# A table for the PSUM banks, the early stage 1 in parts of one pair, 24 single dummy matmuls, and a new order

## The chip, the core and the metric

The kernel runs on one core of a Trainium2 chip. The metric is the time of one execution in microseconds (us), measured on the device; the median over runs counts. The core has five engines that run side by side, each through its own list of instructions in order: PE (TensorE: matmuls, with PEld, the load of the stationary operand, beside it), DVE (VectorE), ACT (ScalarE), POOL (GpSimd) and SP (SyncE, which issues nearly all DMAs here). They wait for each other through semaphores. Matmul results go to PSUM, which has eight banks of 128 x 512 floats; DVE and ACT read them from there.

## The reference

Two layers of attention follow each other, over 8 batches with 576 positions.

```python
scores = scale * np.matmul(q, k.transpose(0, 1, 3, 2))        # 8 heads of 64
mask = (rel >= 0) & (rel < window)                            # window = 64
attn = exp(scores - max); attn /= attn.sum(-1) + 1e-9
x = (attn @ v) laid out as (8, 576, 512)
logits = x @ w_gate                                           # 4 experts, 2 are chosen
for e in range(4):                                            # causal attention of each expert
    a = softmax(scale * (x @ wq[e]) @ (x @ wk[e]).T, causal)
    out += (gate weight of e, or 0) * (a @ (x @ wv[e]) @ wo[e])
```

## The kernel before

**Stage 1** is the windowed attention. Two heads make a pair, so there are 32 pairs, four to a batch. A block of 64 queries sees only its own 64 keys and the 64 before, and eight such blocks of a pair, or of neighbouring pairs, make a unit u; there are 36 units. For a unit, `s1_qk` makes the scores on PE (the tiles s1_u_0 and s1_u_1 in the orders below, two banks), ACT and DVE bring them to SBUF (DVE by `copy_predicated`), DVE takes the row maximum, POOL subtracts it, ACT takes the exponential, DVE the sum and its reciprocal, and POOL multiplies (the tile sm1_u all along, st1_u for maximum, sum and reciprocal). `s1_t` transposes the result on PE (t1_u) and masks it (pt1_u): for the first nine units two of the four masked parts are DVE's and two POOL's, later all four POOL's. `s1_av` multiplies by v on PE (o1_u), and ACT and DVE split the result into a high part xh and a low part xl, so that later products can be made as three fast matmuls. The first 16 blocks come from the first four blocks of each of the four pairs of batch 0, so that the layer behind can begin early.

**Stage 2** is the attention of the experts, two experts at a time (pr = 0, 1). From xh and xl of a batch, PE makes v and the gate's logits (v2ps_b_j), keys and queries (kps_b_pr_half, qps_b_pr_half; 12 matmuls each), then scores (s2_b_pr_k, two banks each), then, after a softmax on DVE, ACT and POOL and a transposition by DVE and DMAs, the product with v (o2_b_pr_part), and last the product with wo (ops_b_j), which ACT or DVE copies out and SP stores. The weights come as 512 KB each and are split by ACT and DVE into parts such as wkhi and wklo before their first use.

**What sets the order.** The functions are first called in an order by planned due times, and each call only records its instructions (`Plan.add`, line 185). A run of matmuls recorded inside one `with nc.block(...)` is one entry; any other instruction is an entry of its own. `Plan.issue` (line 199) then gives the entries out in the order of a table of numbers, `LIST` (lines 29 to 166). All instructions thus have line 203 in the profile. Each engine executes its share of that one order.

**PSUM.** All banks are one pool of eight buffers with one tag. A tile takes the next buffer in turn, in the order in which the functions were called (not the order of `LIST`), and its first matmul waits until the readers of the tile that had the buffer before are done.

**Dummy matmuls.** `warm` (line 540) multiplies the 128 x 128 identity by itself, two matmuls to a call, and there are six calls. The results are not used. They need only `ident`, which POOL makes first.

The change touches `s1_qk` (354), `s1_t` (392), `s1_av` (429), `warm` (540), `s2_v` (546), `proj` (603), `s2_mm` (643), `s2_tp` (714), `s2_av_mm` (778), `s2_o` (808), the pool (225) and the tables.

Of the kernel before, what the change touches and what calls it, by code (L numbers as in the profile page):

```python
# [165 lines left out]
)  # L166
TAIL = 2
WARM = 6
BPOS = 0.05
SJOIN = 1  # L170
PARTS = ((0, 5), (5, 9))
# [797 lines left out]
```

## Time and profile before

| what | value |
|---|---|
| time, median of 3 runs | 412.91 us |
| the runs | 412.62, 412.91, 413.35 us |
| the profiled execution's own time | 413.24 us |
| its span, first to last instruction | 411.5 us |
| PE busy | 398.9 us (97%), 5308 records |
| PEld busy | 358.9 us (87%) |
| DVE busy | 310.7 us (75%) |
| POOL busy | 276.7 us (67%) |
| ACT busy | 260.5 us (63%) |
| moved by DMA | 72.69 MB, 177 GB/s on average |

How to read it: a float32 matmul leaves two records on PE, one of the split parts leaves one. A busy PE is one with a matmul in its pipeline, so short waits between matmuls can hide in it. The time around the span, 413.24 less 411.5 or 1.7 us, is start and end of the execution.

### The profile page before, as it was taken

The page shows a single profiled execution, that of the slowest core. Times are in us where ns is not written, and L with a number is a line of the kernel's source. Part 1 is how long each engine was busy: PE and PEld are TensorE (multiplying, and loading weights), DVE is VectorE, ACT ScalarE, POOL GpSimd, SP SyncE. Part 2 cuts the span into 40 slices and gives each one's busy share as a digit, 9 for nine tenths or more (in the row PEclk, how much of TensorE's full clock was granted, in tenths as well). Part 3 has the DMA queues.
Part 4 walks back from the last instruction along what each step waited for, and adds up shares of the span by engine and source line. Part 5 has one row for each costly group of instructions (what it writes and reads, how often), then busy time and mean ns, then how long its engine had stood idle before and what let it go on. Part 6 is the DMA issues. An engine that isn't in the chain of part 4 may idle for free.

```text
span 411.5 us, 14007 instructions
## 1 busy us (share of the span) xinstructions
PE 398.9 (97%) x5308; PEld 358.9 (87%) x5308; DVE 310.7 (75%) x996; ACT 260.5 (63%) x865; POOL 276.7 (67%) x471
## 2 busy tenths in 40 slices
PE   7689999999999999999999999999999999999996
PEld 7479889999988989898989898988988999898875
DVE  3799998889695878879786876969887768445742
ACT  2666657685748485674858567486856676447852
POOL 3868887977797876887786966877768671504420
PEclk9899999999999999999999999999999999999999
DMA  7987346376867475368776669487657613453113
GB/s 240 349 310 268 111 144 231 78 208 181 239 223 203 135 182 217 106 172 267 193 248 143 205 147 308 130 211 197 176 130 222 151 60 80 131 134 103 53 53 127
DMA packets 33363, 72.69 MB, mean 177 GB/s; under 512 B 6160, under 2 KB 10256, under 8 KB 33296
## 3 DMA queue, kind: packets, MB, share of 16 engines
q1 hardware_dynamic: 32640, 71.14, 58.2%
q8 instruction: 42, 0.69, 0.7%
q10 hardware_dynamic: 656, 0.66, 0.5%
q14 instruction: 25, 0.20, 0.2%
HBM read 39.85 MB, written 9.44 MB: 120 GB/s over the span
## 4 chain that ended last, share of the span: by engine, by line
PE 87%; DVE 8%; POOL 2%; ACT 1%; issue 1%; ACTq 0%; POOLq 0%
PE o L203 18%; PE s L203 17%; PE ops L203 12%; PE v2ps L203 12%; PE kps L203 12%; PE qps L203 11%; PE t L203 4%; DVE pt L203 2%; DVE st L203 2%; DVE sm L203 1%; POOL sm L203 1%; PE warm L203 1%; DVE xl L203 1%; ACT sm L203 0%; DVE wklo L203 0%
## 5 line engine op out<-in xcount | busy, mean ns | idle before, releaser
L203 POOL TENSOR_SCALAR p<-p,r,g 128x448 f32<-128x448 f32 (+4 forms) x135 | 84.0, 636 | 29.5 <-DVE r L203 23.8
L203 POOL TENSOR_TENSOR sm<-sm,st 128x512 f32<-128x512 f32 x72 | 76.9, 1070 | 30.1 <-DVE st L203 20.0
L203 POOL TENSOR_SCALAR_AFFINE_SELECT pt<-ft 64x512 f32<-64x512 f32 x126 | 84.2, 668 | 17.5 <-ACT ft L203 8.4
L203 ACT ACTIVATE p<-p,r 128x192 f32<-128x192 f32 (+3 forms) x135 | 78.7, 588 | 16.9 <-DVE r L203 16.7
L203 PE MATMUL o<-pt,v 128*64 128x64 f32 (+2 forms) x1776 | 80.8, 249 | 1.8 <-DVE pt L203 1.2
L203 PEld LDWEIGHTS o<-pt,v 128*64 128x64 f32 x1776 | 68.2, 138 | 15.0 <-issue 3.2
L203 DVE STREAM_TRANSPOSE st<-p 128x128 f32<-128x128 f32 (+5 forms) x126 | 59.9, 515 | 5.7 <-POOL p L203 5.5
L203 DVE CUSTOM_DVE_ANT_0 p<-s,causal 128x320 f32<-128x320 f32 (+2 forms) x120 | 54.3, 483 | 7.8 <-PE s L203 7.3
L203 DVE TENSOR_REDUCE st<-sm 128x8 f32<-128x512 f32 x72 | 48.4, 679 | 7.0 <-ACT sm L203 6.1
L203 PE MATMUL s<-kt,qt 64*128 64x320 f32 (+3 forms) x480 | 43.3, 318 | 0.0
L203 DVE COPY_PREDICATED sm<-own,s 128x256 f32<-128x256 uint8 x72 | 29.3, 442 | 12.9 <-ACT sm L203 7.7
L203 PE MATMUL kps<-xh,wklo 128*128 128x256 f32 (+1 forms) x128 | 37.7, 295 | 1.2 <-DVE wklo L203 1.2
L203 PE MATMUL kps<-xh,wkhi 128*128 128x256 f32 (+1 forms) x128 | 38.7, 302 | 0.0
L203 PE MATMUL qps<-xh,wqhi 128*128 128x320 f32 (+1 forms) x128 | 38.4, 300 | 0.0
L203 PE MATMUL v2ps<-wvhi,xh 128*128 128x260 f32 x128 | 37.7, 294 | 0.2 <-DVE xl L203 0.2
L203 PE MATMUL s<-k,q 64*64 64x128 f32 (+1 forms) x1116 | 37.8, 275 | 0.1
L203 PE MATMUL qps<-xl,wqhi 128*128 128x320 f32 (+1 forms) x128 | 37.6, 294 | 0.0
L203 PE MATMUL kps<-xl,wkhi 128*128 128x256 f32 (+1 forms) x128 | 37.6, 294 | 0.0
L203 PE MATMUL qps<-xh,wqlo 128*128 128x320 f32 (+1 forms) x128 | 37.6, 294 | 0.0
L203 PEld LDWEIGHTS s<-kt,qt 64*128 64x128 f32 x480 | 35.0, 186 | 2.8 <-issue 0.7
L203 PE MATMUL v2ps<-wvhi,xl 128*128 128x260 f32 x128 | 36.2, 283 | 0.0
L203 PE MATMUL v2ps<-wvlo,xh 128*128 128x260 f32 x128 | 36.2, 283 | 0.0
(124 smaller groups left out, 921.6 us busy)
## 6 DMA issues: line engine op xcount, KB each, us to landing
v<-in_vW_dram SPq DMA_DIRECT2D x28, 576.0 KB, 5.2
pt<-st SPq DMA_DIRECT2D x112, 116.0 KB, 2.3
pt<-st SPq DMA_DIRECT2D x112, 80.0 KB, 2.1
out_dram<-out SPq DMA_DIRECT2D x32, 256.0 KB, 2.5
k<-in_kT_dram SPq DMA_DIRECT2D x28, 288.0 KB, 5.0
q<-in_qT_dram SPq DMA_DIRECT2D x28, 288.0 KB, 5.2
v<-in_vW_dram SPq DMA_DIRECT2D x3, 320.0 KB, 5.9
out_dram<-out SPq DMA_DIRECT2D x7, 128.0 KB, 2.5
```

Of the source, the lines that this page charges most:

```text
L203: call(*args, **kw)
```

## The change

1. The pool has one buffer to a tag and a tag to a bank, and a new table `BANKS` gives the bank's number for each tile, in the order of the calls. `ops` of the last block takes a whole bank and uses half.
2. For the first four units `s1_qk` and `s1_av` record one entry for each pair instead of one for all eight blocks, so that `LIST` can put the parts apart.
3. There are 24 calls of `warm` with one matmul each, instead of six with two.
4. `LIST` is another order of the entries.

```diff
 LIST = (
-    1, 3, 2, 0, 7, 5, 6, 4, 16, 20, 18, 14, 15, 17, 9, 21, 19, 69, 29, 279, 46, 67, 48, 34, 35, 41, 44, 39, 42, 45,
...
+    1441, 1329, 1439, 1391, 1330, 1443, 1251, 1250, 1417, 1393, 1394, 1241, 1309, 1414, 1331, 1310, 1312, 1332, 1311,
...
+BANKS = (
+    "3421040515401232652071113426734076556201052722743234376660505236110176517730416571043232647642412716"
...
-WARM = 6
+WARM = 24
...
-    psum = ctx.enter_context(tc.tile_pool(name="psum", bufs=2, space=PSUM))
+    psum = ctx.enter_context(tc.tile_pool(name="psum", bufs=1, space=PSUM))
+    numbers = iter(BANKS)
+
+    def bank(shape, name):
+        return psum.tile(shape, F32, tag="s" + next(numbers, "0"), name=name)
...
+    def parts(u):
+        t = list(tiles(u))
+        return [[x for x in t if x[2] == p] for p in sorted({x[2] for x in t})] if u < 4 else [t]
+
     def s1_qk(u):
 
-        banks = [psum.tile([128, 4, 128], F32, tag="s", bufs=8, name=f"s1_{u}_{x}") for x in range(2)]
-        with nc.block("s"):
-            for x, j, p, b in tiles(u):
...
+        banks = [bank([128, 4, 128], f"s1_{u}_{x}") for x in range(2)]
+        for group in parts(u):
+            with nc.block("s"):
+                for x, j, p, b in group:
...
     def warm(k):
-        ps = psum.tile([128, 512], F32, tag="s", bufs=8, name=f"warm_{k}")
+        ps = bank([128, 512], f"warm_{k}")
         with nc.block("z"):
-            for i in range(2):
-                nc.tensor.matmul(ps[:, 0:128], lhsT=ident, rhs=ident, start=True, stop=True)
+            nc.tensor.matmul(ps[:, 0:128], lhsT=ident, rhs=ident, start=True, stop=True)
```

In `s1_av` the same loop over `parts(u)` stands around the matmuls. Every other `psum.tile(...)` becomes `bank(...)`. No other instruction is added or taken away.

**The order at the start, on PE.** The first rows of PE before, from the first dummies to the second unit that is multiplied by v:

```order
L203 MATMUL warm_3_103<-ident_85 128x128 x2
L203 MATMUL s1_0_0_106<-k0_74,q0_73 64x64 x2
...
L203 MATMUL warm_4_104<-ident_85 128x128 x2
L203 MATMUL s1_2_0_123<-k0_74,q0_73 64x128 x2
...
L203 MATMUL warm_1_101<-ident_85 128x128 x2
L203 MATMUL t1_0_112<-ident_85,sm1_0_108 128x128 x4
...
L203 MATMUL t1_1_122<-ident_85,sm1_1_115 128x128 x4
L203 MATMUL o1_0_117<-pt1_0_110,v0_79 64x64 x8
L203 MATMUL o1_0_117<-pt1_0_110,v1_80 64x64 x8
L203 MATMUL o1_1_129<-pt1_1_120,v2_81 64x64 x8
L203 MATMUL o1_1_129<-pt1_1_120,st2_69 64x64 x8
L203 MATMUL s1_4_0_146<-st2_69 64x128 x2
```

The same stretch of PE in the changed kernel (k and q are the loaded keys and queries of a pair, v its values, st2 the buffer that holds the fourth pair):

```order
L213 MATMUL warm_18_118<-ident_85 128x128
L213 MATMUL s1_0_0_124<-k0_74,q0_73 64x64 x2
...
L213 MATMUL warm_14_114<-ident_85 128x128
L213 MATMUL s1_3_0_151<-k1_76,q1_75 64x128 x2
L213 MATMUL s1_3_1_152<-k1_76,q1_75 64x128 x2
L213 MATMUL s1_2_1_142<-k1_76,q1_75 64x128 x2
...
L213 MATMUL t1_0_130<-ident_85,sm1_0_126 128x128 x4
...
L213 MATMUL o1_0_135<-pt1_0_128,v1_80 64x64 x8
L213 MATMUL s1_4_0_164<-st2_69 64x128 x2
...
L213 MATMUL t1_2_150<-ident_85,sm1_2_143 128x128 x4
L213 MATMUL o1_1_147<-pt1_1_138,st2_69 64x64 x8
```

Eleven single dummies stand ahead of the first scores where there were eight matmuls, one stands behind unit 0, one inside unit 1, eight behind it and one ahead of t1_0; units 4 and 5, and the transposition of unit 2, have moved ahead of o1_1. Unit 6 and t1_3, not shown, have moved ahead of the first keys (kps).

**The order where DVE last gives PE something to wait for, on PE.** The last matmuls of the first experts' scores and what follows, before (one row of each block; the rest of a block repeats it with other operands):

```order
L203 MATMUL s2_0_0_3_1_250<-kt_0_0_217,qt0_88 128x256
L203 MATMUL v2ps_0_4_268<-wvhi_170,xt0_0_163 128x260
...
L203 MATMUL kps_0_1_1_272<-xh0_118,wkhi_183 128x320
...
L203 MATMUL qps_0_1_1_273<-xh0_118,wqhi_193 128x320
...
L203 MATMUL v2ps_1_1_304<-wvhi_170,xh1_165 128x260
```

And in the changed kernel:

```order
L213 MATMUL kps_0_1_1_290<-xh0_136,wkhi_201 128x320
...
L213 MATMUL s2_0_0_2_0_265<-kt_0_0_235,qt0_88 128x320
...
L213 MATMUL t1_10_0_280<-ident_85,sm1_10_251 128x64
...
L213 MATMUL s2_0_0_3_1_268<-kt_0_0_235,qt0_88 128x256
L213 MATMUL warm_10_110<-ident_85 128x128
L213 MATMUL v2ps_0_4_286<-wvhi_188,xt0_0_181 128x260
...
L213 MATMUL qps_0_1_1_291<-xh0_136,wqhi_211 128x320
...
L213 MATMUL v2ps_1_1_322<-wvhi_188,xh1_183 128x260
```

The second half of the keys (kps_0_1_1), the transposition of unit 10 and one dummy now stand ahead of v2ps_0_4; before, the keys stood right behind it and t1_10 five blocks further on.

**The same place on DVE.** Before, the DVE instructions around the last one that PE has to wait for ahead of v2ps_0_4, which is the copy of unit 11's second bank:

```order
L203 TENSOR_TENSOR gt_0_0_221<-logits0_86,gs_0_0_222 128x16
L203 TENSOR_TENSOR g4_0_0_220<-logits0_86 128x64
L203 COPY_PREDICATED sm1_11_239<-own_82,s1_11_1_238 128x256
L203 ISA p2_1_68,m2_0_0_252<-s2_0_0_2_1_248,causal_98 128x320
L203 ISA m2_0_0_252 128x1
```

In the changed kernel, where the one that v2ps_0_4 waits for is the reading of the scores s2_0_0_2 (the last two rows):

```order
L213 COPY_PREDICATED sm1_11_257<-own_82,s1_11_0_255 128x256
L213 RECIPROCAL st1_10_252<-st1_10_252 128x8
L213 COPY_PREDICATED sm1_11_257<-own_82,s1_11_1_256 128x256
...
L213 COPY_PREDICATED sm1_12_294<-own_82,s1_12_0_292 128x256
...
L213 COPY_PREDICATED sm1_12_294<-own_82,s1_12_1_293 128x256
L213 TENSOR_REDUCE gt_0_0_239<-g4_0_0_238 128x16
L213 ISA p2_1_68,m2_0_0_270<-s2_0_0_2_1_266,causal_98 128x320
L213 ISA m2_0_0_270 128x1
```

Five instructions more stand ahead on DVE: one more copy of unit 11, the two of unit 12, a small reduction of the gate and a reading of scores with its accumulator. The rest of what DVE has done by then is the same in both kernels.

## Rows read from the trace of the kernel before

**Rows 1.** The page's first line.

```profile
span 411.5 us, 14007 instructions
```

**Rows 2.** Windows: stretch and length; busy us of PE, PEld, DVE, ACT, POOL; clock, DMA.

```profile
0.00:10.00 10.00, 7.80 (x103) 7.26 (x105) 3.15 (x12) 2.62 (x7) 3.27 (x20) 1.00 0.79 238
10.00:20.00 10.00, 6.29 (x96) 4.81 (x89) 7.93 (x16) 6.03 (x14) 8.53 (x13) 0.83 0.99 345
20.00:30.00 10.00, 8.19 (x137) 7.53 (x138) 9.88 (x18) 6.60 (x19) 6.50 (x9) 1.00 0.90 342
...
50.00:60.00 10.00, 9.47 (x183) 8.40 (x176) 9.79 (x23) 5.94 (x16) 8.61 (x13) 1.00 0.48 152
```

**Rows 3.** Windows: the stretch from 60 us to 407 us.

```profile
60.00:407.00 347.00, 346.83 (x4460) 312.73 (x4460) 259.88 (x888) 225.28 (x770) 232.62 (x396) 1.00 0.57 164
```

**Rows 4.** Waits of PE, whole span: us in total, times, longest.

```profile
PE t L203 <- POOL sm L203: 3.1, 4, 2.5
PE warm L203 <- POOL ident L203: 2.2, 1, 2.2
PE o L203 <- DVE pt L203: 1.2, 1, 1.2
PE kps L203 <- DVE wklo L203: 1.2, 1, 1.2
...
PE v2ps L203 <- DVE xl L203: 0.2, 1, 0.2
```

**Rows 5.** The chain that ended last, 15 to 60 us: start, length, what.

```profile
24.28 1.55 DVE wklo L203
...
58.25 0.57 DVE xl L203
58.86 1.23 PE v2ps L203 x8
```

**Rows 6.** Waits of DVE between 16 us and 62 us.

```profile
DVE sm L203 <- ACT sm L203: 0.8, 1, 0.8
```

**Rows 7.** Timeline of the first 13 us: start, length, instruction [idle before].

```profile
0.79 0.15 POOL L203 MEMSET sm<- 128x64 f32 x1 [0.29 <-POOLq L955]
...
1.85 0.29 POOL L203 TENSOR_SCALAR_AFFINE_SELECT ident<-ident 128x128 f32<-128x128 f32 x1
...
2.20 3.78 PE L203 MATMUL warm<-ident 128*128 128x128 f32 x16 [2.20 <-POOL ident L203]
...
7.92 0.88 DVE L203 COPY_PREDICATED sm<-own,s 128x256 f32<-128x256 uint8 x2 [2.91 <-PE s L203]
...
9.40 1.26 PE L203 MATMUL s<-k,q 64*64 64x128 f32 x32
...
9.54 0.77 DVE L203 COPY_PREDICATED sm<-own,s 128x256 f32<-128x256 uint8 x2
...
10.60 0.71 PE L203 MATMUL warm<-ident 128*128 128x128 f32 x4
...
12.80 0.64 ACT L203 ACTIVATE sm<-s 128x256 f32<-128x256 f32 x2
```

**Rows 8.** Windows: 14.6 to 18.1 us, with the granted clock third from the end.

```profile
14.60:18.10 3.50, 3.25 (x44) 2.40 (x36) 2.60 (x5) 1.90 (x5) 3.09 (x4) 0.51 1.03 384
```

**Rows 9.** Groups of DVE instructions, 16 to 64 us: busy us, mean ns | idle.

```profile
L203 DVE COPY_PREDICATED sm<-own,s 128x256 f32<-128x256 uint8 x17 | 6.8, 441 | 0.8 <-ACT sm L203 0.8
L203 DVE CUSTOM_DVE_ANT_0 p<-s,causal 128x320 f32<-128x320 f32 x4 | 1.9, 480 | 0.0
L203 DVE TENSOR_REDUCE gt<-g 128x16 f32<-128x64 f32 x1 | 0.2, 208 | 0.0
```

**Rows 10.** Timeline of PE: first matmuls of kps_0_1_1 and qps_0_1_1, and t1_10.

```profile
64.89 0.31 PE L203 MATMUL kps<-xh,wkhi 128*128 128x320 f32 x1
...
66.65 0.31 PE L203 MATMUL qps<-xh,wqhi 128*128 128x320 f32 x1
...
72.49 0.46 PE L203 MATMUL t<-ident,sm 64*128 64x64 f32 x8
```

More of the change, by code (lines that the diff above doesn't have):

```diff
@@ L29 @@
 LIST = (
[136 rows of a table removed]
[138 rows of a table added]
+)
+BANKS = (
+    "3421040515401232652071113426734076556201052722743234376660505236110176517730416571043232647642412716"
+    "1357046213012435126325303140271707261547571563241327604603014317273432710054102565767402443056327654"
+    "1721712274205352526115703646174120320640003414562565374125037624511367652145103715462210451657470132"
+    "5007601243232605324737766274724421304164556413014362315056701731326355071045247161054527462752702416"
+    "0774111645523204467753564237153601417215506727436330117740502433761023413624016074125036772617324264"
+    "1010462351"
 )
 TAIL = 2
-WARM = 6
+WARM = 24
 BPOS = 0.05
@@ L352, in tiles @@
             yield i % 2, i // 2, *ORDER[STARTS[u] + i]
+    def parts(u):
+        t = list(tiles(u))
+        return [[x for x in t if x[2] == p] for p in sorted({x[2] for x in t})] if u < 4 else [t]
     def s1_qk(u):
-        banks = [psum.tile([128, 4, 128], F32, tag="s", bufs=8, name=f"s1_{u}_{x}") for x in range(2)]
-        with nc.block("s"):
-            for x, j, p, b in tiles(u):
-                c0 = 64 * int(b == 0)
-                for h in range(2):
-                    r, o = slice(64 * h, 64 * h + 64), 64 * (h ^ x)
-                    keys = pairs[p][1][r, 64 * b + c0 - 64:64 * b + 64]
-                    nc.tensor.matmul(banks[x][o:o + 64, j, c0:], lhsT=pairs[p][0][r, 64 * b:64 * b + 64],
-                                     rhs=keys, start=True, stop=True)
+        banks = [bank([128, 4, 128], f"s1_{u}_{x}") for x in range(2)]
+        for group in parts(u):
+            with nc.block("s"):
+                for x, j, p, b in group:
+                    c0 = 64 * int(b == 0)
+                    for h in range(2):
+                        r, o = slice(64 * h, 64 * h + 64), 64 * (h ^ x)
+                        keys = pairs[p][1][r, 64 * b + c0 - 64:64 * b + 64]
+                        nc.tensor.matmul(banks[x][o:o + 64, j, c0:], lhsT=pairs[p][0][r, 64 * b:64 * b + 64],
+                                         rhs=keys, start=True, stop=True)
         n, w = SIZES[u], SIZES[u] // 2
@@ L399, in s1_t @@
         if early:
-            ps = psum.tile([128, 4, 128], F32, tag="s", bufs=8, name=f"t1_{u}")[:, :m]
+            ps = bank([128, 4, 128], f"t1_{u}")[:, :m]
             with nc.block("t"):
@@ L405, in s1_t @@
         else:
-            banks = [psum.tile([128, 8, 64], F32, tag="s", bufs=8, name=f"t1_{u}_{o}")[:, :m] for o in range(2)]
+            banks = [bank([128, 8, 64], f"t1_{u}_{o}")[:, :m] for o in range(2)]
             with nc.block("y"):
@@ L431, in s1_av @@
         size, w, start = SIZES[u], SIZES[u] // 2, STARTS[u]
-        o = psum.tile([128, 8, 64], F32, tag="s", bufs=8, name=f"o1_{u}")
-        with nc.block("a"):
-            for i, (x, j, p, b) in enumerate(tiles(u)):
-                for h in range(2):
-                    c = 64 * (h ^ x)
-                    k = x * w + j
-                    nc.tensor.matmul(o[64 * h:64 * h + 64, i], lhsT=pairs[p][2][h, b],
-                                     rhs=t[:, k // 2, k % 2, c:c + 64], start=True, stop=True)
-                if b == BLK - 1 and later(p):
-                    freed.append(p)
+        o = bank([128, 8, 64], f"o1_{u}")
+        for group in parts(u):
+            with nc.block("a"):
+                for x, j, p, b in group:
+                    i = 2 * j + x
+                    for h in range(2):
+                        c = 64 * (h ^ x)
+                        k = x * w + j
+                        nc.tensor.matmul(o[64 * h:64 * h + 64, i], lhsT=pairs[p][2][h, b],
+                                         rhs=t[:, k // 2, k % 2, c:c + 64], start=True, stop=True)
+                    if b == BLK - 1 and later(p):
+                        freed.append(p)
         i = 0
@@ L540, in warm @@
     def warm(k):
-        ps = psum.tile([128, 512], F32, tag="s", bufs=8, name=f"warm_{k}")
+        ps = bank([128, 512], f"warm_{k}")
         with nc.block("z"):
-            for i in range(2):
-                nc.tensor.matmul(ps[:, 0:128], lhsT=ident, rhs=ident, start=True, stop=True)
+            nc.tensor.matmul(ps[:, 0:128], lhsT=ident, rhs=ident, start=True, stop=True)
     def s2_v(b, j):
-        ps = psum.tile([128, 512], F32, tag="s", bufs=8, name=f"v2ps_{b}_{j}")
+        ps = bank([128, 512], f"v2ps_{b}_{j}")
         with nc.block("VW"[j // 4]):
@@ L604, in proj @@
         c0, n = HALVES[b > 0][half]
-        ps = psum.tile([128, 512], F32, tag="s", bufs=8, name=f"{name}ps_{b}_{pr}_{half}")
+        ps = bank([128, 512], f"{name}ps_{b}_{pr}_{half}")
         w = slice(128 * pr, 128 * pr + 128)
@@ L643, in s2_mm @@
     def s2_mm(b, pr, k):
-        banks = SB[b, pr, k] = [psum.tile([128, 512], F32, tag="s", bufs=8, name=f"s2_{b}_{pr}_{k}_{e}")
+        banks = SB[b, pr, k] = [bank([128, 512], f"s2_{b}_{pr}_{k}_{e}")
                                 for e in range(2)]
@@ L725, in s2_tp @@
             s0, w, m = group[0][0], group[0][1].shape[1], len(group)
-            ps = psum.tile([128, 512], F32, tag="s", bufs=8, name=f"t2_{b}_{pr}_{part}_{k}")
+            ps = bank([128, 512], f"t2_{b}_{pr}_{part}_{k}")
             with nc.block("TU"[part]):
@@ L780, in s2_av_mm @@
         n = 64 * (b1 - b0)
-        o = OB[b, pr, part] = psum.tile([128, 512], F32, tag="s", bufs=8, name=f"o2_{b}_{pr}_{part}")
+        o = OB[b, pr, part] = bank([128, 512], f"o2_{b}_{pr}_{part}")
         with nc.block("AB"[part]):
@@ L809, in s2_o @@
         end = b == NB - 1 and j == 4
-        banks = [psum.tile([128, DM // (1 + end)], F32, tag="s", bufs=8, name=f"ops_{b}_{j}_{i}") for i in range(1 + end)]
+        banks = [bank([128, DM], f"ops_{b}_{j}_{i}")[:, 0:DM // (1 + end)] for i in range(1 + end)]
         for letter, prs in (("O", (0, 1)),) if b < NB - 1 else (("o", (0,)), ("O", (1,))):
```

272 rows, old and new, of the table LIST are left out of this document.

## The prediction

> **What bounds the kernel now.** I read the windows first. From 60 us to 407 us PE is busy for 346.8 of 347.0 us, with PEld at 312.7, DVE at 259.9, ACT at 225.3 and POOL at 232.6 [rows 3]. The reader is to see there that this stretch, 84% of the span [rows 1], has one owner: its length is the matmul work that is left at its start. Only the first 60 us can be different. There PE is busy for 7.80, 6.29 and 8.19 us of the first three tens, while DVE goes from 3.15 over 7.93 to 9.88 and is still at 9.79 in the sixth [rows 2].
>
> The list of PE's waits comes next. It names 8.4 us in all; 2.2 of it is the wait for the identity at the very start, and the rest is four kinds of wait: 3.1 for POOL's last step of a unit (one of them 2.5), 1.2 for DVE's pt1, 1.2 for DVE's wklo, and small ones [rows 4]. All lie before 60 us. So PE loses some 6 us in the start, and the question is whether that loss is on the path.
>
> The chain that ended last answers it: between 15 us and 58.8 us it is led back mostly through DVE (wklo at 24.28, an xl at 58.25), and it goes over to PE with v2ps at 58.86 and stays there [rows 5]. In that time DVE waits once, for 0.8 us, for ACT's copy of unit 3 [rows 6]. A DVE that hardly stops cannot be made faster by feeding PE better. PE's holes before 58.86 are mostly time in which PE has done what DVE has prepared; filled at one place, they come back at another. This is the main choice of the forecast.
>
> The Trainium skill ("Perfetto Trace Analysis", Identifying the Most-Contended Engine) says to improve the engine with the highest occupancy first; over the whole span that is PE, with 97% here, and by that the filled holes would count in full, which is the first rival below. The Trainium skill's "Perfetto Trace Analysis", Optimization Strategy, says that a kernel can have stretches with different most-contended engines, and by that it is DVE up to 58.86; these rows agree with the second.
>
> **The change part by part.** The sum is made against the profiled execution's own 413.24 us (span 411.5 and 1.7 around it), which is 0.33 over the median of the runs, 412.91, and within them.
>
> *The front.* The identity is made first on POOL now: before, its last step ran at 1.85, behind memsets and a mask; with only its own memset ahead, POOL's first instruction at 0.79 [rows 7] puts it at about 1.1, so the dummies start some 0.7 us earlier. There are 11 instead of 8 ahead of unit 0. Eight take 3.78 us, 0.47 each [rows 7], eleven 5.2: they end near 6.65 if the clock does not rise earlier, where unit 0 began at about 5.9, and at 5.9 if the rise comes 0.7 us earlier with them. Two more dummies stand between unit 0 and the end of unit 1, at 0.2 to 0.35 us each (two matmuls at the later clock took 0.71) [rows 7]. What is late here is DVE's first copy, 7.92 before [rows 7]. Bounds: 0 and +0.9. I take +0.3.
>
> *The holes of PE.* The 2.5 us hole ahead of t1_0 is filled by nine dummies and by the first part of unit 3; those dummies are no work of the kernel. Into the other two, 1.2 us each, go units 4, 5 and 6 of stage 1. I cost this at nothing, since DVE hides it: PE is then 2.4 us ahead of before and waits for DVE at the next place. If that cover were gone it would be worth 2.4 us.
>
> *DVE's wait of 0.8.* It waits for unit 3, whose scores ran while the granted clock was down: 0.51 on average from 14.6 to 18.1 us [rows 8], the lower of the two levels, after PE had stood still for most of 2.5 us. The new order of DVE has both halves of pt1_0 and the split of wv in that place. Bounds: 0 and -0.8. I take -0.5; the chain over POOL and ACT that feeds DVE there has the same length as before.
>
> *Where DVE lets go.* The last place at which DVE holds PE is near v2ps_0_4. In the changed kernel DVE has five instructions more in front of it: three copies at about 0.40 (17 took 6.8 us), 0.2 for the small reduction, 0.48 for a reading of scores [rows 9], together 1.9, with overlap 1.7. On the other hand PE has done more by then: kps_0_1_1, 64.89 to 66.65, which is 1.76 us, and t1_10, at most 0.46 [rows 10], together 2.1. So PE is let go 1.7 us later with 2.1 us less to do: -0.4, and I take -0.2, because PE can be held one block earlier or later. Bounds: -0.6 and +0.6 (where the earlier blocks, with their own DVE work ahead, decide).
>
> *Dummies in the busy stretch.* One (warm_10) stands right ahead of v2ps_0_4, another (warm_12) among the scores of batch 2. The first is hidden by DVE, the second not: 0.2 to 0.35 us. I take +0.2.
>
> *Banks by table, and the rest of the order.* PE does the same matmuls from 60 us on, and no wait of PE stands there now [rows 3, 4]; the change can only keep that or add to it. A bank is free after its readers, of which DVE copied two in 0.77 us and ACT two in 0.64 at the start [rows 7]; the tables of before leave PE without a wait in some 350 blocks, so a table of any freedom can do no better. Bounds: 0 and +1.5 (a handful of waits of 0.3). I take 0. Nothing is changed in the way out of the last results.
>
> Sum: +0.3 - 0.5 - 0.2 + 0.2 = -0.2, so 413.0 against the profiled execution, and 412.7 against the median. A measurement of this kernel can't tell less than about 0.2%, 0.8 us, from no change.
>
> **The rivals.**
>
> *PE's holes count (faster).* If DVE's busy time is in part work that can be done later, then the new order, which gives PE the units 4, 5 and 6 in the two holes of 1.2 us, takes these 2.4 us off the end: 412.7 - 2.4 = 410.3. For it: PE is the engine that ends the kernel, and DVE has 25% to spare over the whole span. Against it: DVE at 9.79 to 9.88 of 10 us in the tens after 20 us [rows 2], and what is ahead of it at the last place is more in the new order, not less. It would show as a v2ps_0_4 that starts no later than before, with the keys already done.
>
> *The start is held by a bank (slower).* Before, unit 2's scores started at 9.40 right behind a dummy and waited for no one [rows 7]. In the changed kernel units 2 and 3 take banks that DVE has to empty of unit 1 first. DVE's two copies of unit 1 began at 9.54 and took 0.77, so to 10.3 [rows 7]; with +0.3 for the front, unit 3's first part and unit 2 run from 10.6 to about 12.2 (1.26 for unit 2). ACT came to unit 2 at 12.80 [rows 7], so 0.6 us is in hand. The clock decides: at its lower level unit 2 takes twice as long, and everything behind it on DVE is late by about 0.7 to 1.5 us, with nothing to take it up before 58.86. 412.7 + 1.2 = 413.9. For it: eight dummies in a row fill just this time, so the clock may hold; against it too that DVE has other work at 12 to 13 us.
>
> *Waits come into the busy stretch (slower or the same).* The order of some 350 blocks is new. Five new waits of 0.3 us, where a copy by ACT and DVE is late for a bank or for the next product, would give 412.7 + 1.5 = 414.2. For it: the trace of before has none left there, so every deviation costs. Against: the distances on PE between a tile's last matmul and the next one in its bank are of the same kind as before in the order, 1 to 2 us at the shortest.
>
> **How the numbers follow.** My forecast, DVE holds the start and little changes, has a chance of 0.48; the holes count 0.26; the bank at the start 0.13; waits later 0.13. The forecast's own range is from its bounds, taken half together: 411.6 to 413.9. For 8 in 10 I go down to the first rival with half a us of its own spread, 409.8, and up to 414.6, past the last. Faster by over 0.2% is below 412.08: 0.12 from the forecast and 0.25 from the first rival, 0.37. Slower by over 0.2% is above 413.74: 0.05 from the forecast, 0.08 and 0.10 from the two others, 0.23. The rest, 0.40, is no change.
>
> **What would show it.** In the profile of the changed kernel: the dummies' first matmul near 1.5 us and DVE's first copy at 7.9 to 8.8; no wait of PE of 1.2 us for pt1 or wklo any more, but others of a like sum between 20 and 60 us; DVE at 9.7 or more of each ten from 20 to 60 us; v2ps_0_4, before just ahead of the keys that began at 64.89 [rows 10], no earlier than that, with these keys already done; PE at 99% or more from there to its last matmul near 407.5. The forecast is wrong if DVE has more than 2 us of idle time between 20 and 60 us, if v2ps_0_4 starts before 63.5 in spite of the keys ahead of it, or if PE waits for more than 1 us in all behind 66 us.

## The result, and the profile after

The changed kernel takes 415.37 us in the median of 13 runs (413.54 to 415.91), the kernel before 412.78 us in 13 runs beside it (411.81 to 414.20). The ratio, which is taken over all runs of the two and not from the medians, is 1.0053, with a 95% interval of 1.0039 to 1.0067: slower by about half a per cent. The forecast was 412.7 and its range ended at 414.6.

One sentence ahead of the prediction is wrong: before, the eight buffers of PSUM were not given out in the order of the calls. In the compiled program the pool gave the buffers out in the order of `LIST`, and most tiles got the one whose last reader stood furthest back in that order.

The profiled execution of the changed kernel took 414.21 us, 1.0 more than that of before and 1.2 less than its own median. Windows of it, as [rows 2] and [rows 3]: stretch, length; busy us of PE, PEld, DVE, ACT, POOL; granted clock, DMA share, GB/s.

```profile
0.00:10.00 10.00, 8.57 (x93) 7.59 (x94) 2.52 (x8) 2.25 (x7) 3.39 (x21) 1.00 0.77 238
10.00:20.00 10.00, 7.64 (x156) 6.30 (x158) 8.89 (x19) 7.35 (x16) 7.79 (x10) 1.00 1.02 354
20.00:30.00 10.00, 7.43 (x140) 6.51 (x132) 9.84 (x20) 5.35 (x18) 9.02 (x13) 1.00 0.88 333
...
40.00:50.00 10.00, 10.00 (x174) 9.45 (x169) 8.56 (x21) 5.88 (x19) 8.79 (x15) 1.00 0.66 220
50.00:60.00 10.00, 8.61 (x156) 8.07 (x158) 9.74 (x25) 4.85 (x16) 7.47 (x13) 1.00 0.09 35
60.00:407.00 347.00, 346.18 (x4457) 311.62 (x4453) 256.60 (x887) 224.72 (x769) 233.29 (x397) 1.00 0.58 166
```

The clock holds at 1.00 where it fell to 0.83 before, and PE is busier up to 20 us, partly with dummies. DVE now has 1.44 us of idle time between 40 and 50 us, and PE loses 1.39 us in the ten after. The long stretch, which had 0.17 us of idle PE, now has 0.82. The waits of PE, us in total, times, longest, as [rows 4]:

```profile
PE t L213 <- POOL sm L213: 2.4, 3, 1.4
PE o L213 <- POOL pt L213: 1.7, 3, 1.1
PE warm L213 <- POOL ident L213: 1.4, 1, 1.4
PE v2ps L213 <- DVE wvlo L213: 1.1, 1, 1.1
PE o L213 <- DVE pt L213: 1.1, 1, 1.1
PE t L213 <- DVE gt L213: 0.4, 1, 0.4
PE o L213 <- DVE sm L213: 0.3, 1, 0.3
```

The sum is 8.4 us, as before, at other places. The two last rows are new in kind: they lie at 241 and 239 us, in the stretch that had no wait.

A split that needs no averaging: qps_0_1_1 stands behind all work of the start in both kernels, and ops_7_0_0 near the end; the matmuls between them are the same but for t1_10 (0.46 us), which stands behind qps_0_1_1 in the kernel before alone, and a dummy in the changed kernel. PE's first matmul of each, before:

```profile
66.65 0.31 PE L203 MATMUL qps<-xh,wqhi 128*128 128x320 f32 x1
...
397.97 0.48 PE L203 MATMUL ops<-wohi,y7xh 128*128 128x512 f32 x1
```

and in the changed kernel:

```profile
66.87 0.31 PE L213 MATMUL qps<-xh,wqhi 128*128 128x320 f32 x1
...
399.01 0.40 PE L213 MATMUL ops<-wohi,y7xh 128*128 128x512 f32 x1
```

So the start is 0.22 later, and the busy stretch 332.14 us instead of 331.32. Below, "start" and "stretch" are these two numbers for each run. One profile is one draw: the four with the changed order all the way and no mend behind 66 us give a stretch of 332.1 to 334.2. The start varies too: two profiles of the old start have 66.65 and 65.75.

### The profile page after: what moved, and what is told of

It is laid out like the page before. It is cut to its first block, busy times and chain, and to the rows that moved or that the text cites. A ratio compares the mean times of both kernels' runs of the same rounds, so it can differ in the third digit from the quotient of the medians.

```text
span 412.5 us, 14068 instructions
## 1 busy us (share of the span) xinstructions
PE 400.0 (97%) x5332; PEld 360.0 (87%) x5332; DVE 306.4 (74%) x996; ACT 259.5 (63%) x865; POOL 275.8 (67%) x471
## 4 chain that ended last, share of the span: by engine, by line
PE 89%; DVE 6%; POOL 2%; ACT 1%; issue 1%; POOLq 0%; ACTq 0%
PE o L213 18%; PE s L213 16%; PE ops L213 13%; PE v2ps L213 12%; PE kps L213 12%; PE qps L213 12%; PE t L213 4%; DVE st L213 2%; PE warm L213 1%; POOL sm L213 1%; DVE sm L213 1%; DVE pt L213 1%; ACT sm L213 1%; POOL pt L213 1%; DVE wvlo L213 0%
## 5 line engine op out<-in xcount | busy, mean ns | idle before, releaser
L213 POOL TENSOR_TENSOR sm<-sm,st 128x512 f32<-128x512 f32 x72 | 75.8, 1055 | 24.4 <-DVE st L213 15.7
L213 ACT ACTIVATE p<-p,r 128x320 f32<-128x320 f32 (+4 forms) x135 | 78.1, 582 | 9.2 <-DVE r L213 9.1
L213 DVE STREAM_TRANSPOSE st<-p 128x128 f32<-128x128 f32 (+5 forms) x126 | 61.1, 518 | 11.5 <-POOL p L213 7.1
L213 DVE COPY_PREDICATED sm<-own,s 128x256 f32<-128x256 uint8 x72 | 30.4, 438 | 15.1 <-ACT sm L213 12.7
L213 PE MATMUL kps<-xh,wkhi 128*128 128x320 f32 (+1 forms) x128 | 38.8, 303 | 0.0
L213 PE MATMUL kps<-xl,wkhi 128*128 128x320 f32 (+1 forms) x128 | 37.6, 294 | 0.0
L213 PE MATMUL kps<-xh,wklo 128*128 128x320 f32 (+1 forms) x128 | 37.6, 294 | 0.0
L213 PE MATMUL s<-k,q 64*64 64x128 f32 (+1 forms) x1116 | 36.6, 269 | 0.0
L213 ACT ACTIVATE ft<-t 128x256 f32<-128x256 f32 (+1 forms) x63 | 24.3, 415 | 19.1 <-PE t L213 10.8
```

The source lines that it names most:

```text
L213: call(*args, **kw)
```

## The experiments

Theory at first: the start is worth about nothing, and the changed order of the busy stretch loses the time. Rivals: the table of banks; the start; and, later, a loss in a few places against one spread over the order. All hybrids keep every instruction but the dummies; only the order differs. "Pool" means one tag of eight buffers as before: a_pool, the runs with h and those with m have it, a_fix1, a_mend_rest and a_mend_all keep the table. The rows come from several series, in which the kernel before had 412.56 to 412.87, so the ratio is the safer column.

| run | median us | ratio to before (95%) | start | stretch |
|---|---|---|---|---|
| before (first profile) | 412.78 | 1 | 66.65 | 331.32 |
| changed | 415.37 | 1.0053 (1.0039 to 1.0067) | 66.87 | 332.14 |
| a_pool | 415.13 | 1.0071 (1.0047 to 1.0095) | 66.61 | 333.14 |
| h1_old_start | 414.75 | 1.0061 (1.0037 to 1.0086) | 65.75 | 333.10 |
| h2_new_start | 411.92 | 0.9984 (0.9965 to 1.0003) | 67.06 | 331.34 |
| a_fix1 | 414.68 | 1.0054 (1.0031 to 1.0078) | 66.18 | 334.16 |
| a_mend_rest | 416.96 | 1.0089 (1.0066 to 1.0113) | 66.70 | 334.55 |
| a_mend_all | 415.59 | 1.0067 (1.0042 to 1.0091) | 65.43 | 334.74 |
| h2_fix1 | 411.07 | 0.9960 (0.9934 to 0.9986) | 66.08 | 330.50 |
| h2_fix1_b (again) | 411.14 | 0.9959 (0.9941 to 0.9977) | 65.42 | 330.21 |
| h2_fix2 | 412.47 | 0.9996 (0.9978 to 1.0015) | 66.03 | 330.20 |
| h2_11dum | 412.57 | 0.9983 (0.9968 to 0.9998) | 65.77 | 330.74 |
| h2_fix1_11 | 411.80 | 0.9976 (0.9955 to 0.9998) | 65.67 | 330.27 |
| m_early | 415.59 | 1.0066 (1.0041 to 1.0091) | 65.19 | 333.98 |
| m_early2 | 412.33 | 0.9989 (0.9972 to 1.0006) | 65.88 | 331.53 |
| m_mid | 413.77 | 1.0029 (1.0016 to 1.0042) | 65.65 | 332.97 |
| m_late | 411.63 | 0.9980 (0.9961 to 0.9999) | 65.82 | 331.77 |
| m_mid_mend | 418.91 | 1.0148 (1.0118 to 1.0179) | 65.30 | 337.88 |

**The table or the order.**

```diff
-    psum = ctx.enter_context(tc.tile_pool(name="psum", bufs=1, space=PSUM))
+    psum = ctx.enter_context(tc.tile_pool(name="psum", bufs=2, space=PSUM))
...
-        return psum.tile(shape, F32, tag="s" + next(numbers, "0"), name=name)
+        return psum.tile(shape, F32, tag="s", bufs=8, name=name)
```

> The changed kernel's order and its 24 dummies, with PSUM as in the kernel before: one tag of eight buffers, handed out by the pool, instead of the table. Before is 412.8 us, the changed kernel 415.4 in the median and 414.2 in its profiled execution. Theory 'order' (the order loses the time: a late chain at 47 to 58 us, two late products near 240 us, a dummy): the table is worth nothing, 414.7 to 415.7, and PE still waits near 54 and near 240 us. Rival 'table' (banks bound too early by the table make PE wait): 412.8 to 413.8, with the waits near 101, 144 and 240 us gone.

415.13, as the theory has it: the table is worth nothing that can be measured (the intervals overlap). The waits near 239 and 241 us are there too; one of 0.5 us near 188 us is new, for a bank that ACT had not yet read. It is in the profiles of h1_old_start and m_mid as well, and in neither of the changed kernel and a_fix1: it belongs to the pool with this order.

**Start or rest.** The orders are cut behind the matmuls of v2ps_0_4.

```diff
 h1_old_start:
-    up to v2ps_0_4: the changed order, 23 dummies
+    up to v2ps_0_4: the order before, its 12 dummies
 h2_new_start:
-    behind v2ps_0_4: the changed order, a dummy
+    behind v2ps_0_4: the order before, no dummy
```

> The kernel before up to v2ps_0_4 (its order and its 12 dummies), the changed order behind it, banks by the pool, the dummy in the scores of batch 2 left out. Theory 'rest' (the start of both is worth the same; what the changed kernel loses it loses behind 66 us, some 0.8 us of it near 240 us): 413.8 to 415.4. Rival 'start' (the new start costs it): 412.4 to 413.3, like before.

> The changed kernel up to v2ps_0_4 (its order and 23 of its dummies), the order before behind it, banks by the pool. Theory 'rest': 412.5 to 413.4. Rival 'start': 414.5 to 415.5. If both parts cost: this one and the one with the old start lie between and their differences to before add up to the changed kernel's 2.4.

The old start with the changed rest is slow, the new start with the old rest is not; whether it is faster than before is not clear of the noise. So the loss is made behind 66 us. The stretch column says the same: 331.3 with the old rest, 333.1 with the new one.

The order before is not free of waits in every run either. The profiled run of h2_new_start was its slowest (413.66), and PE waited in it for ACT, which had waited for a store of the results:

```profile
168.46 0.60 ACT L213 ACTIVATE out<-ops 128x512 f32<-128x512 f32 x1 [1.91 <-DMA out_dram<-out]
...
169.11 0.61 PE L213 MATMUL s<-k,q 64*64 64x128 f32 x8 [0.84 <-ACT out L213]
```

**The start's one bad place.** In the changed kernel ACT's copy of unit 10's scores needs the buffer of unit 7, which t1_7 has to read; ACT's small step of unit 8 stands behind it, and DVE waits for that step. Timeline of the changed kernel: start, length, instruction, idle time before it and what ended it.

```profile
47.41 0.66 PE L213 MATMUL t<-ident,sm 128*128 128x128 f32 x4
...
48.16 0.39 ACT L213 ACTIVATE sm<-s 128x256 f32<-128x256 f32 x1 [1.17 <-PE t L213]
48.44 0.20 ACT L213 ACTIVATE st<-st 128x8 f32<-128x8 f32 x1
48.68 0.20 DVE L213 RECIPROCAL st<-st 128x8 f32<-128x8 f32 x1 [1.21 <-ACT st L213]
...
54.80 0.69 DVE L213 TENSOR_TENSOR pt<-t,tri 64x512 f32<-64x512 f32 x1
55.64 0.92 PE L213 MATMUL o<-pt,v 128*64 128x64 f32 x24 [1.10 <-DVE pt L213]
```

The 1.2 us that DVE loses at 47.5 come out on PE at 54.5, in o1_7. The mend, on ACT and on DVE:

```diff
 L213 ACTIVATE sm1_9_247<-s1_9_1_246 128x256
+L213 ACTIVATE st1_8_220<-st1_8_220 128x8
 L213 ACTIVATE sm1_10_251<-s1_10_0_249 128x256
-L213 ACTIVATE st1_8_220<-st1_8_220 128x8
...
 L213 RECIPROCAL st_8_220<-st_8_220 128x8
+L213 TENSOR_TENSOR pt_6_198<-t_6_200,tri 64x4x128
 L213 COPY_PREDICATED sm_10_251<-own,s_10_0_249 128x256
 L213 TENSOR_TENSOR xl_184<-o_5_196,xh_183 128x512
-L213 TENSOR_TENSOR pt_6_198<-t_6_200,tri 64x4x128
```

> The changed kernel with two instructions moved: ACT's small step of unit 8's sum (st1_8) ahead of its copy of unit 10's scores, which waits until t1_7 has read the buffer; and DVE's second half of pt1_6 ahead of its copy of unit 10. Theory 'chain': DVE's wait of 1.2 us at 47.5 us goes down to some 0.3, PE's wait of 1.1 us for pt1_7 near 55 us goes, and all behind comes 0.9 to 1.3 us earlier: 414.1 to 414.5 where the changed kernel has 415.4. Rival 'DVE's sum' (DVE's whole work sets when PE is let go, and the wait comes back at v2ps_0_4): 415.0 to 415.6, with a wait of PE of about 1 us between 56 and 66 us instead.

414.68 lies between the two; the trace decides for the chain as far as the start goes. Waits of DVE and then of PE between 40 and 66 us, with the mend:

```profile
DVE sm L213 <- ACT sm L213: 0.3, 1, 0.3
DVE xl L213 <- ACT xh L213: 0.3, 1, 0.3
DVE p L213 <- PE s L213: 0.2, 1, 0.2
```

```profile
PE o L213 <- POOL pt L213: 0.3, 1, 0.3
PE o L213 <- DVE pt L213: 0.2, 1, 0.2
```

The start is 66.18, 0.7 earlier. By all the profiles that is more than the spread: 66.6 to 67.1 in four without the mend, 65.2 to 66.2 in eleven with it, ten of which also leave out the dummy ahead of v2ps_0_4 (0.24 us). This profile lost it again in the stretch, at two places that had not waited in the changed kernel's own profile:

```profile
206.70 1.65 PE L213 MATMUL o<-pt,v 128*64 128x256 f32 x24 [1.05 <-DMA k<-in_kT_dram]
...
255.34 0.85 PE L213 MATMUL o<-pt,v 128*64 128x256 f32 x11 [0.75 <-DVE gt L213]
```

The named releasers are not the cause: by the program's order these are o2_2_1_0 and o2_3_1_0, and each began 0.14 and 0.20 us after the last DMA that stores its transposed softmax (pt) had landed. How long such stores take is in the DMA view, for those issued between 200.9 and 202.9 us here, and between 200 and 202.9 us in the changed kernel (KB each, us from issue to landing):

```profile
pt<-st SPq DMA_DIRECT2D x2, 116.0 KB, 4.4
pt<-st SPq DMA_DIRECT2D x2, 80.0 KB, 4.9
```

```profile
pt<-st SPq DMA_DIRECT2D x3, 116.0 KB, 2.9
pt<-st SPq DMA_DIRECT2D x2, 80.0 KB, 3.5
```

Over a whole run the medians are 2.3 and 2.1. So the landing of one group differs by 1.4 to 1.5 us between these two runs, and an order that leaves less room can wait in one run and not in another. Room of o2 behind its last landed store, before: 0.27 us at o2_2_1, 1.31 at o2_3_1, over 2 at all others; changed: 0.20 at o2_3_1, 0.14 at o2_5_1, 1.1 at o2_2_1 and o2_6_0. This would fit that the changed kernel's median is 1.2 over its one profiled run, but no run shows that it is the reason.

**A few places, or no room?** In the first mend three blocks that were long ready are set ahead of those that waited.

```diff
 a_mend_rest, PE:
+o1_23
 o2_2_1
-o1_23
...
+kps_4_1_0
 t1_27
-kps_4_1_0
...
+s2_4_1_0
 o2_3_1
-s2_4_1_0
```

> The changed kernel with its banks, start and all else, but three blocks of PE in the busy stretch set in front of a product that the traces saw waiting: o1_23 ahead of o2_2_1 (which waited 1.04 us for a late store in one profile, not in another), kps_4_1_0 ahead of t1_27 (0.55 in each, for POOL), s2_4_1_0 ahead of o2_3_1 (0.5 to 0.7 in two of four, for a store); the dummy in batch 2's scores left out. Theory 'places' (the loss of the rest sits in a few places where a product stands too near to its store or its last POOL step): 413.6 to 414.5, and no wait of PE over 0.4 us at these places. Rival 'everywhere' (the new order has less room all along; what is mended here comes back at the next place): 414.9 to 415.6.

> The kernel of the run above with the mend of the start too (ACT's st1_8 and DVE's half of pt1_6 moved, the dummy ahead of v2ps_0_4 left out). Theory 'places': 412.8 to 413.8. Rival 'everywhere': 414.2 to 415.2, as with the start's mend alone.

The theory "places" fell in both, and the times lie beyond the ranges of the rival too: 416.96, 1.6 slower than the changed kernel. The waits that were mended are gone, and others stand right behind them: 0.5 us at 243.9 for ACT's copy of t1_27, which has become late, 0.4 us at 247.2 for a bank that the moved kps_4_1_0 had taken. With the start's mend too it is 415.59, 1.4 better again (the range of the rival ended at 415.2).

Which part of the stretch loses? With the new, mended start, one part at a time in the changed order.

```diff
 order behind v2ps_0_4:
-    the order before
+    m_early:  changed up to o2_1_1 (154 us), then the order before
+    m_early2: changed up to ops_0_1 (113 us), then the order before
+    m_mid:    changed from o2_1_1 to the scores s2_5_0 (286 us) alone
+    m_late:   changed behind the scores s2_5_0 alone
```

> The new start with its mend, and of the busy stretch only the part from v2ps_0_4 to o2_1_1 (some 66 to 154 us) in the changed order; behind it the order before. Banks by the pool, no dummy behind 60 us. With the order before all the way this was 411.1 us, with the changed order all the way some 414.7. Theory 'middle' (the loss is made between o2_1_1 and the scores of batch 5, some 154 to 286 us, where all waits of PE were seen): 410.8 to 411.5. Rival 'everywhere' (each third costs a third): 412.0 to 412.5.

> The same with only the part from o2_1_1 to the scores s2_5_0 (some 154 to 286 us) in the changed order. Theory 'middle': 412.8 to 414.5, with waits of PE near 188, 206, 240 and 254 us, 1 to 2.5 us in all. Rival 'everywhere': 412.0 to 412.5.

> The same with only the part behind the scores s2_5_0 (286 us to the end) in the changed order. Theory 'middle': 410.8 to 411.5. Rival 'everywhere': 412.0 to 412.5. If it is over 412.5 the loss is made near the end (the wait of 0.65 us ahead of the last transpositions near 390 us).

> As the run with the early part of the busy stretch in the changed order, which waited 2.4 us right behind its seam for pt1_18, so that its time says little on the part itself. Here the seam is at some 113 us, where the two orders have done nearly the same. Theory 'middle': 410.8 to 411.9. Rival 'everywhere': 412.3 or more. A wait of over 0.5 us right behind 113 us would be a seam again.

m_early, far beyond both ranges, waited 2.0 us right at its seam, for pt1_18 of POOL, and says little. Against the same kernel with the order before (411.1): m_early2 +1.2, m_mid +2.7, m_late +0.5, where the intervals of m_late and h2_fix1_b overlap. So the middle costs most, as its theory had it, but "middle alone" is not right either: m_early2 is in the range of the rival, m_late between the two. The stretch is 331.5, 333.0 and 331.8 against 330.2 to 330.7. The parts add up to more than the whole, and what a part costs can't be told from what its seam costs.

The traces themselves part the stretch without a seam. At o2_1_1, s1_26 and qps_6_1_1 (near 152, 197 and 330 us) PE has done the same matmuls in both orders, and the same block comes next. From place to place, with the program's order laid beside the trace, in us, mean and range of the profiles:

| part | order before (7) | changed order (4) |
|---|---|---|
| 67 to 152 | 85.4 (85.4 to 85.7) | 85.8 (85.6 to 86.0) |
| 152 to 197 | 44.8 (44.6 to 45.8) | 44.7 (44.4 to 45.2) |
| 197 to 330 | 132.1 (131.8 to 132.4) | 134.4 (133.6 to 135.6) |
| 330 to 398 | 68.3 | 68.2 |

qps_6_1_1, before and in the changed kernel:

```profile
329.65 0.28 PE L203 MATMUL qps<-xh,wqhi 128*128 128x256 f32 x1
...
330.81 0.28 PE L213 MATMUL qps<-xh,wqhi 128*128 128x256 f32 x1
```

So 2.3 of the 2.5 us are lost between 197 and 330 us, and 1.9 of them from 239 to 287 us, again between places with the same matmuls done. The windows of that piece, before, in h2_fix1_b and in the changed kernel:

```profile
238.79:286.53 47.74, 47.64 (x645) 43.08 (x644) 36.27 (x127) 31.66 (x109) 35.16 (x65) 1.00 0.74 208
236.97:284.19 47.22, 47.22 (x645) 42.88 (x645) 36.30 (x127) 31.64 (x109) 35.22 (x65) 1.00 0.73 207
238.82:287.58 48.76, 48.33 (x645) 43.36 (x647) 37.77 (x133) 31.82 (x110) 36.29 (x63) 1.00 0.67 186
```

The same 645 matmuls take longer, and only 0.43 us of it is idle time of PE; its busy time is 0.7 to 1.1 us longer. Over the whole stretch it is like this, here for h2_fix1_b and h1_old_start:

```profile
65.42:395.63 330.21, 330.14 (x4276) 298.74 (x4274) 251.91 (x854) 216.94 (x740) 228.86 (x388) 1.00 0.58 167
65.75:398.85 333.10, 331.28 (x4277) 298.77 (x4274) 246.22 (x849) 216.03 (x739) 227.86 (x387) 1.00 0.57 163
```

With the changed order PE is idle for 0.8, 1.5, 1.8 and 2.6 us of the stretch in the four profiles, and busy for 331.3 to 331.6; with the order before it is idle for 0.04 to 0.9 in seven, and busy for 330.1 to 330.5 in the six that have t1_10 ahead of it. So of the 2.5 us some 1.5 are waits and 1.0 a longer busy time. Some of the latter are tenths at blocks that have another neighbour in the changed order (kps_5_0_0 takes 1.87 us instead of 1.75, but o1_29 0.93 instead of 1.03), and 0.3 is the dummy among the scores of batch 2 where it stands; no run takes the tenths away, so what they cost in all is not shown.

Of m_late's profile, 0.8 us of the 1.1 over the mean of the order before are there by 286 us, where it still has that order, with the wait of ACT for a store as above (0.42 us on PE at 167). m_early2 loses its part between 67 and 152 us, 86.8 where the changed order all the way has 85.6 to 86.0, so most of it comes with the cut and not with that order.

Waits of PE behind 60 us in m_mid:

```profile
PE o L213 <- ACT ft L213: 0.5, 1, 0.5
PE t L213 <- DVE gt L213: 0.4, 1, 0.4
PE o L213 <- DVE sm L213: 0.3, 1, 0.3
```

They lie at 188, 240 and 238 us, and the first of them is the pool's, as in a_pool. In m_early2 and m_late no wait there stands above 0.5 us. The two others are tied to POOL: t1_26 stands at 232.4 us where it stood at 221.3, so POOL's four masks of unit 26 run from 235.2 to 238.4, and its last steps of units 28 and 27, 1.05 us each, come behind them. In the changed kernel:

```profile
240.11 1.05 POOL L213 TENSOR_TENSOR sm<-sm,st 128x512 f32<-128x512 f32 x1
...
241.22 0.53 PE L213 MATMUL t<-ident,sm 64*128 64x64 f32 x8 [0.43 <-DVE gt L213]
```

POOL ends at 241.16, PE's t1_27 begins at 241.22; the DVE that the row names had been done.

The last try gives such blocks more to stand behind, with the pool:

```diff
 m_mid, PE:
+kps_4_1_0
 o1_26
-kps_4_1_0
...
+qps_4_1_1
 t1_27
-qps_4_1_1
...
+v2ps_3_3
 o2_2_0_0
-v2ps_3_3
...
+o1_23
 o2_2_1
-o1_23
```

> The run with the middle part in the changed order (413.8), with blocks that were long ready set ahead of those that waited: kps_4_1_0 ahead of o1_26, qps_4_1_1 ahead of t1_27, v2ps_3_3 ahead of o2_2_0_0, o1_23 ahead of o2_2_1. Banks by the pool, so that a moved block takes whatever bank is free. Theory 'places': 412.2 to 413.0, the waits of 0.5 us at 188 and 240 us gone. Rival 'no room' (a wait that is mended comes back at the blocks behind, as with the banks by the table): 413.5 to 414.5, with waits at other blocks between 180 and 265 us.

418.91, far beyond either expectation. Timeline of the place:

```profile
244.23 0.66 ACT L213 ACTIVATE ft<-t 128x256 f32<-128x256 f32 x2 [2.27 <-PE t L213]
...
244.96 2.80 POOL L213 TENSOR_SCALAR_AFFINE_SELECT pt<-ft 64x512 f32<-64x512 f32 x4 [2.79 <-ACT ft L213]
...
247.80 0.39 ACT L213 ACTIVATE ft<-t 128x256 f32<-128x256 f32 x1
...
248.23 2.18 PE L213 MATMUL s<-k,q 64*64 64x128 f32 x36 [2.23 <-ACT ft L213]
```

t1_27 is later by the moved blocks; ACT copies it at 244.23 into the one buffer that there is (ft), POOL's four masks hold that buffer until 247.76, ACT's copy of t1_28 waits for it, and s1_31 waits for the bank of t1_28. The theory "no room" is borne out at this place, though not in its size: a product that is set later makes the chain behind it late, by more than it saved.

**The start by itself.**

```diff
 h2_new_start:
+    the mend of ACT's st1_8 and DVE's pt1_6           (h2_fix1, h2_fix1_b)
+    the mend, and s1_11 ahead of o1_8                 (h2_fix2)
+    only the 11 dummies ahead of unit 0               (h2_11dum)
+    the mend, and only these 11 dummies               (h2_fix1_11)
-    the dummy ahead of v2ps_0_4                       (all four)
```

> The new start with its mend (ACT's st1_8, DVE's half of pt1_6, no dummy ahead of v2ps_0_4), the order before behind it, banks by the pool. Theory: the new start was worth 0.8 us, its mend 0.7 to 1.3 more: 410.4 to 411.4, faster than before by 0.3 to 0.6 per cent. Rival 'DVE's sum' (the start can't be made shorter by mending one wait): 411.6 to 412.3.

> The new start with its mend and the order before behind it, once more, for its interval: 410.7 to 411.6.

> The new start with its mend and one more: s1_11 ahead of o1_8, which waited 0.65 us for POOL's pt1_8 in each profile; the order before behind it, banks by the pool. If PE sets the end from 55 us on: 410.4 to 410.8, 0.5 under the kernel without this move (411.1). If DVE still holds v2ps_0_4: no less than 411.0.

> The new start with only its 11 dummies ahead of unit 0, the 12 others left out (so PE has holes where they stood), the order before behind it, banks by the pool. Theory 'dummies hold the clock': the granted clock falls to about 0.5 for some us between 10 and 20 us, units 2 and 3 take up to twice as long, DVE waits 0.5 to 1 us for them: 412.3 to 413.2, against 411.9 with all. Rival 'dummies do nothing': 411.5 to 412.1, the clock at 1.00 or its fall without a wait of DVE.

> The same with only the 11 dummies ahead of unit 0. In the profile without the 12 others, and without the mend, PE was 1.6 us ahead at 28 us, the granted clock stayed at 1.00, and at 60 us little of the lead was left. Theory 'DVE holds the start': the lead is lost again, 410.8 to 411.7. Rival 'the dummies cost': 409.8 to 410.6.

The mended start with the order before behind it is faster than both kernels, by 0.4% in two series, as expected, and behind 60 us the list of PE's waits is empty again. The window of h2_fix1_b:

```profile
60.00:405.00 345.00, 344.93 (x4421) 311.15 (x4413) 259.48 (x883) 224.84 (x767) 232.04 (x394) 1.00 0.58 166
```

In h2_fix2 the 0.3 us that o1_8 waited came back as waits of 0.2 to 0.3 for DVE ahead of two blocks of scores and of kps_0_1_1, and the start did not move (66.03): there DVE does hold PE, as the prediction argued. Its median, 412.47, is 1.3 above the kernel without that move, and its interval does not meet that of h2_fix1_b; its one profile, of a fast run (411.50), does not show where, with a stretch of 330.20 and no wait behind 67 us. That stays open.

The profile of h2_11dum, without the 12 dummies, has a granted clock of 1.00 although PE stood still for two thirds of 10 to 13 us:

```profile
10.00:13.00 3.00, 0.87 (x20) 0.66 (x20) 1.95 (x5) 1.90 (x5) 2.14 (x4) 1.00 1.00 348
13.00:16.00 3.00, 2.13 (x32) 1.48 (x32) 2.87 (x7) 2.23 (x6) 2.71 (x5) 1.00 1.03 384
```

It is the odd one. Of the 12 runs of h2_11dum the 11 others have a mean granted clock of 0.990 to 0.992, and all 12 of h2_fix1_11 have 0.990 to 0.994, where 12 of the 13 runs of the changed kernel have 0.998 to 1.000. The profile of h2_fix1_11 shows the fall, to the lower of the clock's two levels:

```profile
10.00:13.00 3.00, 0.74 (x20) 0.50 (x19) 1.92 (x6) 1.61 (x5) 2.14 (x4) 0.96 1.02 349
13.00:16.00 3.00, 2.35 (x28) 1.88 (x28) 2.45 (x6) 1.71 (x5) 2.79 (x4) 0.50 1.05 374
16.00:19.00 3.00, 3.00 (x44) 2.49 (x36) 2.94 (x6) 2.99 (x7) 1.47 (x3) 0.50 1.07 391
```

So the dummies do hold the clock, which is what the run was to tell: without them the mean was down in 23 of 24 runs. The fall did not make the start later in this profile (65.67, against 65.2 to 66.2 with them), and by the ratios the two pairs are 0.9983 against 0.9984 and 0.9976 against 0.9959, with intervals that overlap. So the worth of the 12 dummies in time stays open.

## Why the prediction was wrong

*The step that failed* is "Banks by table, and the rest of the order", taken at 0 with bounds of 0 and +1.5. The stretch costs 2.5 us on the mean of the profiles (332.1, 333.1, 333.1 and 334.2 with the changed order, 330.2 to 331.3 in seven with the order before), and 2.5 by the ratio of the run with the old start, 2.3 of it between 197 and 330 us. The half on the banks was right as far as can be measured: a_pool and the changed kernel are the same. The half on the order had the sign right ("can only keep that or add to it") and then took the lower end of its range, for no other reason than that no wait stood there before. The third rival named the result's kind, new waits in the busy stretch, at 414.2 and a chance of 0.13. It looked at the wrong resource: it compared distances of blocks in the same bank. What the traces show in its place is, in part, less room of products behind POOL's last steps and masks, and behind stores whose landing varies: the room in the old order could have been read from the trace before, that in the new order only guessed. That gives the waits, some 1.5 of the 2.5 us. The other 1.0 is a longer busy time of PE over the same matmuls, and its cause stays open.

The signs that the prediction named for being wrong did not fire, though the time lies outside its range: in this one profile DVE was idle for 2.0 us between 20 and 60 us (the limit was more than 2), v2ps_0_4 began at 65.34, and PE was idle for 0.8 us behind 66 us (the limit was 1). Only DVE's 8.56 of 10 us from 40 on was less than the 9.7 it asked for. The sum of the waits was not the whole measure for the stretch.

*The front*, +0.3: the first dummy at 1.43, as said, and DVE's first copy at 8.15 instead of 7.92, +0.2. Right.

*The holes*, 0: the waits for pt1 and wklo at 19 and 26 us went and others of a like sum came, 1.1 for wvlo and 1.7 for pt1. Up to 60 us PE idles for 7.75 us, after 8.53, but that counts the dummies as work. The better sign is the start, 66.87 after 66.65, which did not come 2.4 us earlier: in the sum, right. What the filled holes are worth by themselves no run parts from the other terms.

*DVE's wait of 0.8*, -0.5: it went, but DVE lost 1.2 us at 47.5, a chain that the prediction did not follow, though the order shows it: ACT's step behind a copy that waits for t1_7. Its mend and the dummy ahead of v2ps_0_4 together are worth about 1 us of the start, so the term is wrong by about that much.

*Where DVE lets go*, -0.2: v2ps_0_4 began at 65.34, with kps_0_1_1 done, as said; the work behind it began 0.22 later than before. In this trace PE came without a wait from 58.7 on, so it was not DVE that held it there, but the chain before.

*Dummies in the busy stretch*, +0.2: two of them held the block behind for 0.24 and 0.31 us, and the one ahead of v2ps_0_4, taken as hidden, was not. Too small by some 0.3.

The start's terms together, -0.4, are not far from what the new start measures, 0.9984 (0.9965 to 1.0003) or -0.7 us, but with one term off by about 1 us and an interval that takes in 0 that is luck as much as aim.

What stays open: what makes PE's busy time longer, between 239 and 287 us above all. And the parts of POOL and of the stores were seen in traces, but neither was taken away by itself.

## What to carry to other kernels

A stretch in which PE never waits can still be made slower by an order. Where to look is read from the room: for each product, how long ago its last producer was done, and for DMAs how much that landing varies between runs. The price is not in the waits of one profile: here they came to 0.8 us in one and 2.6 in another, and a longer busy time over the same matmuls came on top. When an order is exchanged, cut the two at a place where both have done the same work and measure both hybrids; here that parted a start that cost nothing, and with its mend gained 0.4%, from a rest that cost more. And before further cuts, look in the traces at hand for places where both orders have done the same work: the time from one to the next has no seam in it. A wait in a full chain is not mended by setting its block later; follow what that block feeds first.

## What was not expected of the hardware

Stores of 80 to 116 KB landed after 2.1 to 2.3 us in the median, but after 4.4 to 4.9 in one group of one profile, and after 2.9 to 3.5 in the same group of another. The granted clock stayed at 1.00 in one run through a hole that left PE busy for 0.87 of 3 us, and fell to 0.50 in another run behind a hole alike (0.74 of 3 us). By the mean granted clock it fell in 23 of the 24 runs without the 12 dummies. In the old start's hybrid it was 0.59 between 19 and 22 us, after PE had been busy for 1.02 us of the three before. One profile does not tell what the clock does in most runs.
